# Reordering the first batch of a cross-attention and feed-forward kernel: attention ahead of weights, and idle-time products on the array

## The chip, the cores and the metric

One core of a Trainium2 chip (trn2). The metric is the device time of one execution in microseconds, lower is better. A run of 3 or 5 rounds executes the kernel and the kernel before by turns on the same chip. Runs are compared by their ratios to the kernel before.

## The reference

Eight batches of attention between `x` (8 heads, 512 tokens, 64 wide) and a state of 32 tokens, read in both directions, then a feed-forward block over all 8 x (512 + 32) tokens.

```python
scores = scale * x @ state.T;  a  = softmax(scores);   xread = a @ state      # per batch and head
scores2 = scale * state @ x.T; a2 = softmax(scores2);  sread = a2 @ x
x2 = concat([xread, sread], tokens)            # heads side by side: 512 wide
h  = x2 @ w_in                                 # 512 -> 2048
sp = softplus(h)
out = (h * erf(sp)) @ w_out                    # 2048 -> 512
```

`w_in` and `w_out` come to the kernel as 64-bit numbers, so the kernel must turn them into 32-bit ones itself.

## The kernel before

The weights are loaded in pieces of 1 MB. Each piece costs two ScalarE and three VectorE passes, and these stand among everything else that the first batch asks of the two engines.

```python
def weight(dst, src, shape, tag, bufs):
    raw = act.tile([P, 2 * shape[0] * i], U32, name=tag, bufs=bufs)
    nc.sync.dma_start(out=raw..., in_=src.bitcast(U32))
    lo, hi = words[:, :, 0], words[:, :, 1]
    nc.scalar.activation(out=dst, in_=hi.bitcast(F32), func=ACTF.Copy, scale=2.0 ** -112)
    nc.scalar.activation(out=lo, in_=lo, func=ACTF.Copy, scale=2.0 ** -29)
    nc.vector.tensor_scalar(d, d, 3, None, op0=ALU.logical_shift_left)
    nc.vector.tensor_tensor(d, d, lo, op=ALU.add)
    nc.vector.scalar_tensor_tensor(out=d, in0=hi, scalar=0x80000000, in1=d, ...)

def weights_in(g):                 # two pieces: 256 rows of w_in by 512 columns
    ... weight(..., "raw", 2)
def weights_out(g):                # two pieces; their raw tiles share tag "hs" with hidden()
    ... weight(..., "hs", 2)
```

The attention's output itself is not formed: `mixed` multiplies the states into `w_in` (tile `m`), and `hidden` multiplies the attention weights `aT` by it. A group is four rows of 128 hidden columns.

```python
def hidden(b, fts, t0, n):
    hs = act.tile([P, 4, S], F32, name="hs")
    s = act.tile([P, 4, S], F32, name="s")
    for i in range(4):                                   # four "hidden rows"
        hp = ps_h.tile([P, S], F32, name="h")            # PSUM, two buffers
        ... two matmuls of 128x512 ...
        nc.scalar.activation(out=s[:, i, :], in_=hp, func=ACTF.Softplus)
        nc.vector.tensor_copy(hs[:, i, :], hp)           # frees hp
    nc.scalar.activation(out=s, in_=s, func=ACTF.Erf)
    nc.vector.tensor_tensor(s, s, hs, op=ALU.mult)       # "the product"

load_st(nc.scalar, slice(0, 1))      # eight small loads
load_x(0)                            # eight loads, all on sync's queue
states(0)
rest = attention(0)                  # rest: the read of the states, side work
for b in range(B + 1):
    for g, (first, second) in enumerate(groups):
        if b == 0:
            weights_in(g); mixed(0, g); weights_out(g)
        ...
        gT = first()                 # hidden
        if b == 0 and g == 0:
            rest()
        if pending is not None:
            pending()                # projection of the group before
```

A scheduler settles the order of each engine's instructions; what is written in the program only bounds it.

Of the kernel before, what the change touches and what calls it, by code (L numbers as in the profile page):

```python
# [8 lines left out]
F32 = mybir.dt.float32  # L9
U32 = mybir.dt.uint32  # L10
ALU = mybir.AluOpType
ACTF = mybir.ActivationFunctionType
# [4 lines left out]
def kernel(  # L17
# [17 lines left out]
    nc = tc.nc  # L35
    B, H, S, D = x.shape
    Ns = state.shape[2]
    d_model, d_ff = moe_w_in.shape
    P = 128
    NI = H // 2  # L40
    NC = S // P
    NK = d_model // P
    NF = d_ff // P
    GF = 4
    NG = NF // GF
    TB = S + Ns
    scale = 1.0 / (D ** 0.5)
# [3 lines left out]
    const = ctx.enter_context(tc.tile_pool(name="const", bufs=1))  # L51
# [14 lines left out]
    x_t = {}  # L66


    def load_x(b):
        t = xin.tile([P, NC, H, D], F32, name="x")  # L70
        for h in range(H):
            nc.sync.dma_start(out=t[:, :, h, :], in_=x[b, h].rearrange("(p c) d -> p c d", c=NC))
        x_t[b] = t


    st = const.tile([P, B, P], F32, name="st")

    def load_st(queue, bs):
        for h in range(H):
            i, e = h // 2, h % 2  # L80
            queue.dma_start(out=st[Ns * i:Ns * i + Ns, bs, D * e:D * e + D],
                            in_=state[bs, h].rearrange("b n d -> n b d"))

    load_st(nc.scalar, slice(0, 1))
    load_x(0)

    w_in = const.tile([P, NG, NK, GF * P], F32, name="w_in")
    w_out = const.tile([P, NF, d_model], F32, name="w_out")

    def weight(dst, src, shape, tag, bufs):  # L90
# [20 lines left out]

    gw = GF * P

    def weights_in(g):
        fs = slice(gw * g, gw * g + gw)
        for k in range(0, NK, 2):
            weight(w_in[:, g, k:k + 2, :],
                   moe_w_in[P * k:P * k + 2 * P, fs].rearrange("(k p) f -> p k f", p=P),
                   (2, gw), "raw", 2)

    def weights_out(g):
        for t in range(GF * g, GF * g + GF, 2):
            weight(w_out[:, t:t + 2, :],
                   moe_w_out[P * t:P * t + 2 * P].rearrange("(t p) e -> p t e", p=P),
                   (2, d_model), "hs", 2)


    sT = const.tile([P, NK, B, Ns], F32, name="sT")
# [3 lines left out]
    def states(b):  # L132

        ps = ps_at.tile([P, P], F32, name="at")
        nc.tensor.transpose(out=ps, in_=st[:, b, :], identity=ident)
        stT[b] = keep.tile([P, P], F32, name="stT")
        nc.scalar.copy(stT[b], ps)

    def attention(b):

        xt = x_t.pop(b)
        xT = att.tile([P, NI, S], F32, name="xT")
# [14 lines left out]
                                 start=True, stop=True)  # L157
        sc = att.tile([P, 2, S], F32, name="sc")
        for e in range(2):
            nc.scalar.copy(sc[:, e], s2[e])  # L160

        both = att.tile([P, NI, S], F32, name="xT")
        a = both[:, 0:2].rearrange("p e (k n) -> p e k n", n=Ns)
        aT[b] = keep.tile([P, 2, S], F32, name="aT")
        for e in range(2):
            s1 = ps_at.tile([P, NC * NI, Ns], F32, name="at")
            for c in range(NC):
                nc.tensor.transpose(out=s1[:, NI * c:NI * c + NI, :],  # L168
                                    in_=sc[:, e, P * c:P * c + P], identity=ident)
            m1 = small.tile([P, NC * NI], F32, name="m1")  # L170
            nc.vector.reduce_max(out=m1, in_=s1, axis=AX.X)
            nc.vector.tensor_tensor(a[:, e], s1, m1.unsqueeze(2).to_broadcast([P, NC * NI, Ns]),
                                    op=ALU.subtract)
            nc.scalar.activation(out=a[:, e], in_=a[:, e], func=ACTF.Exp, scale=scale)
            z1 = small.tile([P, NC * NI], F32, name="z1")
            nc.vector.reduce_sum(out=z1, in_=a[:, e], axis=AX.X)
            nc.vector.tensor_scalar(z1, z1, 1e-9, None, op0=ALU.add)
            nc.vector.reciprocal(z1, z1)
            nc.vector.tensor_tensor(a[:, e], a[:, e],
                                    z1.unsqueeze(2).to_broadcast([P, NC * NI, Ns]), op=ALU.mult)  # L180

        for e in range(2):
            ps = ps_at.tile([P, S], F32, name="at")
# [37 lines left out]
            nc.tensor.transpose(out=ps, in_=sn, identity=ident)  # L221
            nc.scalar.copy(sT[:, :, b, :], ps)

        return rest

    m_t = {}

    def mixed(b, g):

        mg = mix.tile([P, 2, gw], F32, name="m")  # L230
        ps = [ps_at.tile([P, gw], F32, name="at") for _ in range(2)]
        for i in range(NI):
            for e in range(2):
                r, q = slice(D * e, D * e + D), slice(Ns * i, Ns * i + Ns)
                nc.tensor.matmul(out=ps[e][q, :], lhsT=stT[b][r, q],  # L235
                                 rhs=w_in[r, g, i, :], start=True, stop=True)
        nc.scalar.copy(mg[:, 0], ps[0])  # L237
        nc.vector.tensor_copy(mg[:, 1], ps[1])  # L238
        m_t[b, g] = mg

    def hidden(b, fts, t0, n):



        hs = act.tile([P, 4, S], F32, name="hs")
        s = act.tile([P, 4, S], F32, name="s")
        m = S // n
        for i in range(4):
            hp = ps_h.tile([P, S], F32, name="h")
            for j in range(m):  # L250
                ops = pairs(b, fts[m * i + j], slice(t0, t0 + n))
                for k, (lhsT, rhs) in enumerate(ops):
                    nc.tensor.matmul(out=hp[:, n * j:n * j + n], lhsT=lhsT, rhs=rhs,  # L253
                                     start=(k == 0), stop=(k == len(ops) - 1))
            nc.scalar.activation(out=s[:, i, :], in_=hp, func=ACTF.Softplus)  # L255
            nc.vector.tensor_copy(hs[:, i, :], hp)  # L256
        nc.scalar.activation(out=s, in_=s, func=ACTF.Erf)  # L257
        nc.vector.tensor_tensor(s, s, hs, op=ALU.mult)  # L258
        return s, hs

    def project(gT, g, acc):
        for r in range(NC):
# [87 lines left out]
    def pairs(b, f, toks):  # L350
        g, fs = f // GF, slice(P * (f % GF), P * (f % GF) + P)
        if b < B:
            return [(m_t[b, g][:, e, fs], aT[b][:, e, toks]) for e in range(2)]
        return [(w_in[:, g, k, fs], sT[:, k].rearrange("p b n -> p (b n)")[:, toks])
                for k in range(NK)]

    def tiles(n):
# [2 lines left out]
    def plain(b):  # L360

        box = []

        def project_(g, gT):
            if g == 0:
                box.extend(tiles(NC))
            project(gT, g, box)
            if g == NG - 1:
                store(box, lambda r, ot: put_x(b, r // 2)(r % 2, ot))
        for g in range(NG):  # L370
            yield lambda g=g: hidden(b, range(GF * g, GF * g + GF), 0, S)[0], \
                lambda gT, g=g: project_(g, gT)

    def fast(b, parts, put):

        for h in range(parts):
            box = []

            def project_(gT, k, g, h, box):
                if k == 0:  # L380
                    box.extend(tiles(4))
                project7(*gT, g, k == 0, k == 1, box)
                if k == 1:
                    store7(box, put(h))
            for k in range(2):
                g = k ^ (h & 1)
                yield lambda g=g, h=h: hidden(b, range(2 * GF * g, 2 * GF * g + 2 * GF),
                                              2 * P * h, 2 * P), \
                    lambda gT, k=k, g=g, h=h, box=box: project_(gT, k, g, h, box)

    states(0)
    rest = attention(0)
    pending = last = None
    for b in range(B + 1):
        if b == 0:
            groups = plain(b)
        elif b < B:
            groups = fast(b, 2, lambda h, b=b: put_x(b, h))
        else:
            groups = fast(b, 1, lambda h: put_s)  # L400
        for g, (first, second) in enumerate(groups):
            if b == 0:
                weights_in(g)
                mixed(0, g)
                weights_out(g)
                if g == 1:
                    load_st(nc.sync, slice(1, B))
            if b + 1 < B and g == (1 if b == 0 else 0):
                load_x(b + 1)
                states(b + 1)  # L410
            gT = first()
            if b == 0 and g == 0:
                rest()
            if pending is not None:
                pending()
            if last is not None:
                last()
                last = None
            if b == 0 and g == NG - 1:
                last = combine_w()  # L420

            def pending(gT=gT, second=second):
                second(gT)
            if b + 1 < B and (b or g):
                for i in [g] if b or g > 1 else [0, 1]:
                    mixed(b + 1, i)
                if g == (NG - 1 if b == 0 else 1):
                    attention(b + 1)()
    pending()


# [28 lines left out]
```

## Time and profile before

| | before |
|---|---|
| median of 3 (lowest to highest) | 817.22 us (816.39 to 817.23) |
| span of the profiled execution | 816.1 us |
| mean granted clock | 0.981 |
| TensorE busy | 784.9 us |
| first projection starts | 55.74 us |

PE is TensorE, DVE is VectorE, ACT is ScalarE. A line of the profile in order of time has the start in us, the busy us, the engine, the source line, the operation, output and input tiles and their sizes, the number of records, and in brackets the idle time before it with what ended that. A matmul of 32-bit numbers leaves two records. The prediction below shows the slices, windows, waits and the start; these lines of the same view (TensorE alone) go beside those of the changed kernel:

```profile
33.46 5.44 PE L253 MATMUL h<-aT,m 128*128 128x512 f32 x8 [0.72 <-ACT m L237]
...
39.45 3.70 PE L253 MATMUL h<-aT,m 128*128 128x512 f32 x8
...
50.56 5.34 PE L253 MATMUL h<-aT,m 128*128 128x512 f32 x8
```

Each line is two hidden rows. They take 3.70 us at full clock; at 33.46 and at 50.56 the clock is at half for most or part of them, 5.44 and 5.34.

### The profile page before, as it was taken

How to read it: one execution, taken by the hardware profiler on the slowest of the kernel's cores; microseconds unless marked ns; L12 is line 12 of the kernel's file. 1: busy time of each engine (PE TensorE's matmuls, PEld its weight loads, DVE VectorE, ACT ScalarE, POOL GpSimd, SP SyncE). 2: the span in 40 equal slices, each digit the busy share in tenths (PEclk: the TensorE clock that was granted, in tenths of full speed). 3: DMA queues.
4: the chain of work that ended last, by engine and by line, in shares of the span. 5: the costliest groups of instructions: out<-in, count | busy, mean ns of one | idle time of the engine just before them, and what ended most of it. 6: DMA issues, size and time to landing. Idle time of an engine off the chain costs nothing.

```text
span 816.1 us, 10344 instructions
## 1 busy us (share of the span) xinstructions
PE 784.9 (96%) x4384; PEld 598.3 (73%) x4384; DVE 429.0 (53%) x625; ACT 370.4 (45%) x465; POOL 0.7 (0%) x6
## 2 busy tenths in 40 slices
PE   4589999999999999999999999999999999999997
PEld 2233434778888788878887888878887788888886
DVE  1979765438444554556453844555454745443431
ACT  4778444545333833345333633373334533333220
POOL 0000000000000000000000000000000000000000
PEclk8589999999999999999999999999999999999999
DMA  7578200202000020002000110000000000000000
GB/s 262 158 231 251 77 27 33 72 1 46 33 1 27 1 78 1 27 1 78 1 27 0 25 55 1 26 1 27 1 26 1 27 1 27 1 27 0 26 1 26
DMA packets 45485, 35.26 MB, mean 43 GB/s; under 512 B 36992, under 2 KB 36992, under 8 KB 45440
## 3 DMA queue, kind: packets, MB, share of 16 engines
q1 hardware_dynamic: 45056, 34.55, 13.6%
q8 instruction: 34, 0.56, 0.3%
q10 hardware_dynamic: 384, 0.07, 0.0%
q14 instruction: 11, 0.09, 0.0%
HBM read 25.69 MB, written 8.91 MB: 42 GB/s over the span
## 4 chain that ended last, share of the span: by engine, by line
PE 88%; ACT 5%; DVE 3%; DMA 3%; issue 1%; SPq 0%
PE o L317 44%; PE h L253 30%; PE at L235 4%; PE o L264 4%; DMA hs<-in_moe_w_out_dram 1%; PE at L168 1%; PE at L146 1%; PE at L185 1%; ACT L255 1%; PE at L202 1%; PE at L214 1%; DMA raw<-in_moe_w_in_dram 1%; ACT s L255 1%; DVE s L258 1%; ACT s L257 0%
## 5 line engine op out<-in xcount | busy, mean ns | idle before, releaser
L253 PE MATMUL h<-aT,m 128*128 128x256 f32 (+1 forms) x960 | 243.4, 401 | 1.9 <-ACT m L237 1.8
L253 PEld LDWEIGHTS h<-aT,m 128*128 128x128 f32 x960 | 178.8, 191 | 67.2 <-issue 33.7
L256 DVE COPY hs<-h 128x512 f32<-128x512 f32 x136 | 93.4, 690 | 198.2 <-ACT s L255 198.2
L255 ACT ACTIVATE s<-h 128x512 f32<-128x512 f32 x136 | 80.3, 597 | 170.9 <-PE h L253 170.5
L258 DVE TENSOR_TENSOR s<-s,hs 128x2048 f32<-128x2048 f32 x34 | 77.9, 2292 | 77.1 <-ACT s L257 77.1
L317 PE MATMUL o<-raw,hs 128*128 128x256 f32 x480 | 115.7, 380 | 0.0
L317 PE MATMUL o<-w_out,s 128*128 128x256 f32 x480 | 115.0, 379 | 0.0
L317 PE MATMUL o<-w_out,hs 128*128 128x256 f32 x480 | 113.4, 379 | 0.0
L317 PEld LDWEIGHTS o<-w_out,hs 128*128 128x128 f32 x480 | 91.2, 190 | 12.4
L317 PEld LDWEIGHTS o<-w_out,s 128*128 128x128 f32 x480 | 90.2, 190 | 12.6 <-DVE s L258 0.8
L317 PEld LDWEIGHTS o<-raw,hs 128*128 128x128 f32 x480 | 90.2, 190 | 12.3
L237 ACT COPY m<-at 128x512 f32<-128x512 f32 x32 | 18.7, 584 | 155.4 <-PE at L235 155.4
L257 ACT ACTIVATE s<-s 128x2048 f32<-128x2048 f32 x34 | 65.0, 1911 | 0.4
L264 PE MATMUL o<-w_out,s 128*128 128x512 f32 x128 | 58.8, 598 | 0.0
L317 PE MATMUL o<-T,s 128*128 128x256 f32 x240 | 56.7, 379 | 0.0
L255 ACT ACT_TABLE_LOAD x41 | 52.6, 1283 | 0.7
L317 PEld LDWEIGHTS o<-T,s 128*128 128x128 f32 x240 | 45.1, 190 | 5.9
L238 DVE COPY m<-at 128x512 f32<-128x512 f32 x32 | 22.1, 690 | 45.6 <-PE at L235 45.5
L264 PEld LDWEIGHTS o<-w_out,s 128*128 128x128 f32 x128 | 23.4, 190 | 30.4 <-issue 30.3
L257 ACT ACT_TABLE_LOAD x34 | 43.6, 1283 | 0.6
L235 PE MATMUL at<-w_in,stT 64*32 64x512 f32 x512 | 41.6, 630 | 0.9 <-ACT m L237 0.5
L328 ACT COPY m<-o 128x256 f32<-128x256 f32 x15 | 5.6, 372 | 57.7 <-PE o L317 57.7
(71 smaller groups left out, 556.4 us busy)
## 6 DMA issues: line engine op xcount, KB each, us to landing
x<-in_x_dram SPq DMA_DIRECT2D x64, 128.0 KB, 3.1
raw<-in_moe_w_in_dram SPq DMA_DIRECT2D x8, 1024.0 KB, 6.1
hs<-in_moe_w_out_dram SPq DMA_DIRECT2D x8, 1024.0 KB, 5.0
out_dram<-ot SPq DMA_DIRECT2D x32, 256.0 KB, 2.4
out_dram<-ot SPq DMA_DIRECT2D x8, 64.0 KB, 1.7
st<-in_state_dram SPq DMA_DIRECT2D x8, 56.0 KB, 4.9
st<-in_state_dram ACTq DMA_DIRECT2D x8, 8.0 KB, 2.1
```

What stands on the lines that cost most here:

```text
L146: nc.tensor.transpose(out=xp[:, P * c:P * c + P], in_=xt[:, c, 2 * i:2 * i + 2, :], identity=ident)
L168: nc.tensor.transpose(out=s1[:, NI * c:NI * c + NI, :], in_=sc[:, e, P * c:P * c + P], identity=ident)
L235: nc.tensor.matmul(out=ps[e][q, :], lhsT=stT[b][r, q], rhs=w_in[r, g, i, :], start=True, stop=True)
L237: nc.scalar.copy(mg[:, 0], ps[0])
L238: nc.vector.tensor_copy(mg[:, 1], ps[1])
L253: nc.tensor.matmul(out=hp[:, n * j:n * j + n], lhsT=lhsT, rhs=rhs, start=(k == 0), stop=(k == len(ops) - 1))
L255: nc.scalar.activation(out=s[:, i, :], in_=hp, func=ACTF.Softplus)
L256: nc.vector.tensor_copy(hs[:, i, :], hp)
L257: nc.scalar.activation(out=s, in_=s, func=ACTF.Erf)
L258: nc.vector.tensor_tensor(s, s, hs, op=ALU.mult)
L264: nc.tensor.matmul(out=acc[r], lhsT=gT[:, i, P * r:P * r + P], rhs=w_out[:, GF * g + i, :], start=(g == 0 and i == 0), stop=(g == NG - 1 a ...
L317: nc.tensor.matmul(out=acc[bank][:, E2 * c:E2 * c + E2], lhsT=lhs[:, i, :], rhs=rhs[:, g, i, :], start=(first and i == 0 and c == 0), stop ...
```

## The change

The intent is to shorten the start: x comes on two queues; attention goes ahead of the weights' conversions by fixed orders; `w_in` comes in pieces that hold all rows of 256 columns, so that half a mixed product needs one piece; thirty products that nobody reads keep the array busy; the side work `rest()` goes from the first group to the third.

```diff
-    def load_x(b):
+    def load_x(b, queues=(nc.sync,)):
...
+    for e in range(2):
+        nc.sync.dma_start(out=st[:, 0, D * e:D * e + D], in_=state[0].rearrange(...)[e])
+    load_x(0, (nc.scalar, nc.sync))
-    load_st(nc.scalar, slice(0, 1))
-    load_x(0)
...
-    def weights_in(g):           # two pieces per group, each 256 rows x 512 columns
+    def weights_in(j):           # one piece: 512 rows x 256 columns
...
+    def warm(n):
+        for _ in range(n):
+            nc.tensor.matmul(out=spare[:, 0:P], lhsT=ident, rhs=ident, start=True, stop=True)
...
+    def begin(on_pe, on_act, on_dve):        # called in attention, behind the subtractions
+        with tc.issue_after(on_pe.ins):
+            warm(20)
+        with tc.issue_after(on_act.ins), tc.issue_after(on_dve.ins):
+            weights_in(0)
+
+    warm(10)
     states(0)
-    rest = attention(0)
+    rest, on_act, on_dve = attention(0, begin)
+    with tc.issue_after(on_act.ins), tc.issue_after(on_dve.ins):
+        weights_in(1)
+    on_act, on_dve = mixed(0, 0, 2)
+    with tc.issue_after(on_act.ins), tc.issue_after(on_dve.ins):
+        weights_out(0)
...
-            gT = first()
-            if b == 0 and g == 0:
-                rest()
+            before, gT = gT, first()
+            if b == 0 and g == 2:
+                with tc.issue_after(before[2].ins):
+                    rest()
```

Cut: the loop's bookkeeping, `mixed` in parts, and the later loads of x and states. `issue_after` sets an order on an engine, not a wait for the result.

## The prediction

> **What bounds the kernel now.** I read the page's forty slices first, then busy time in 20 us windows, then what TensorE waited for, then the start in order of time. Slices (one is 20.4 us):
>
> ```profile
> PE   4589999999999999999999999999999999999997
> DVE  1979765438444554556453844555454745443431
> ACT  4778444545333833345333633373334533333220
> PEclk8589999999999999999999999999999999999999
> ```
>
> TensorE is full from the fourth slice on; only the first three have room, and there its clock is low and VectorE is at 9, 7, 9. Windows (columns: stretch and length, busy us of PE, PEld, DVE, ACT, POOL, clock, DMA share, GB/s):
>
> ```profile
> 0.00:20.00 20.00, 8.52 (x41) 4.84 (x41) 3.30 (x4) 8.45 (x12) 0.70 (x6) 0.83 0.80 266
> 20.00:40.00 20.00, 11.44 (x39) 4.73 (x39) 19.31 (x31) 14.31 (x18) 0.00 (x0) 0.58 0.47 146
> 40.00:60.00 20.00, 17.74 (x112) 7.47 (x111) 15.89 (x20) 15.62 (x20) 0.00 (x0) 0.83 0.80 246
> 60.00:80.00 20.00, 19.15 (x75) 6.75 (x73) 18.35 (x20) 16.84 (x17) 0.00 (x0) 1.00 0.78 247
> ```
>
> TensorE is idle 11.48 + 8.56 + 2.26 = 22.3 us before 60 us. From 20 to 40 VectorE works 19.31 of 20. TensorE's waits up to 130 us:
>
> ```profile
> PE at L185 <- DVE xT L179: 7.7, 2, 7.0
> PE at L135 <- DMA st<-in_state_dram: 6.6, 1, 6.6
> PE at L156 <- ACT xT L148: 3.8, 1, 3.8
> PE h L253 <- ACT m L237: 1.8, 2, 1.1
> ```
>
> And the start:
>
> ```profile
> 13.85 1.12 ACT L105 ACTIVATE w_in<-raw 128x1024 f32<-128x1024 f32 x1 [3.51 <-DMA raw<-in_moe_w_in_dram]
> 14.86 0.58 ACT L148 COPY xT<-at 128x512 f32<-128x512 f32 x1
> 17.49 1.07 ACT L160 COPY sc<-at 128x512 f32<-128x512 f32 x2 [1.00 <-PE at L156]
> 20.75 1.28 DVE L172 TENSOR_TENSOR xT<-at,m 128x512 f32<-128x512 f32 x2
> 38.08 0.60 ACT L255 ACTIVATE s<-h 128x512 f32<-128x512 f32 x1 [0.28 <-PE h L253]
> 48.26 2.29 DVE L258 TENSOR_TENSOR s<-s,hs 128x2048 f32<-128x2048 f32 x1 [1.32 <-ACT s L257]
> 55.74 2.74 PE L264 MATMUL o<-w_out,s 128*128 128x512 f32 x6
> ```
>
> The reader sees ScalarE held 3.51 us by a weight transfer while the last xT copy stands behind it; the first Softplus at 38.08; the first projection at 55.74. After that TensorE lacks only 0.39 + 0.46 + 1.11 + 0.48 us up to 140.
>
> **The Trainium skill.** "TensorE: Matmul & The Clock Gate", Part 1, says the array runs at half clock after a little-used window of about 3.4 us, full after a busy one, the windows running freely. The trace agrees: full to 13.1, half to 37.0, full to 47.2, half to 54.0, distances of 7, 3 and 2 times 3.41. The same page (Architectural detail) says ScalarE and VectorE queues are strictly first in, first out; the 3.51 us above is that. "DMA: Bandwidth & Descriptors" (Issuing engines are not separate DMA queues) says a second issuer saves only issue time; here eight x issues take 6.51 us on one queue, so issue is what limits x. "ScalarE: Activation LUTs" (What ACT_TABLE_LOAD costs) gives 1283 ns; the page's rows show 1283.
>
> **The change, part by part.** I compared the order of instructions on each engine and which instruction each wait is for. From the second batch on the orders are the same, so only the first batch can move. As units I take distances from one start to the next in the trace: ScalarE conversion 1.02 (two per 1 MB piece), VectorE's three per piece 0.60 + 1.13 + 1.13 = 2.86, copies and reductions 0.60, a hidden matmul instruction 0.86 at full clock and 1.72 at half, a 1 MB load 5.07 from issue to landing.
>
> x on two queues, state in two loads instead of eight. Four x issues go on ScalarE (0.65 each, done by 3.3), four on sync behind two state loads; two of these wait for an earlier transfer's semaphore, so the last x lands near 8.1 (3.1 after issue) against 10 now. The first w_in piece follows it by 3.9 as now: 12.0.
>
> Attention ahead. Last xT copy 8.75 instead of 14.86, scores copied at 10.4 to 11.4, both subtractions done at 14.05 instead of 22.03: eight us won. But the fixed order only says "not before"; the built order puts the first piece's two ScalarE conversions (12.0 to 14.1) before the exponentials, and its three VectorE passes between the sums. Chain: exponentials 14.1 to 15.2, pass 14.0, sum, pass 15.3, sum, pass 17.1, scalings to 20.1. Two transposes and aT copies end near 22.3 (now 30.7).
>
> Finer w_in. The first mixed half needs one piece, but its two sides use one PSUM buffer in turn: m halves ready near 22.4 and 23.7, hidden matmuls from about 23.1 (now 33.46). ScalarE must convert the third piece first: its raw buffer comes free at 18.4, so landed 23.5, converted 25.5, table 26.8. The three hidden matmuls ahead of the second mixed half end at about 28.1 at half clock. First Softplus there, ten us earlier than 38.08.
>
> Here the gain is given back. w_out's two pieces, converted before the first hidden matmul now, come after the mixed copies, and the hidden copy needs a buffer which they hold. From T = 28.1: Softplus and m copy to 29.1, four ScalarE conversions to 33.2, VectorE behind them (third and second-last passes), first hs copy ended at 35.9. The third hidden row can't start before; TensorE idles about 6 us, falls to half clock, and ends row four near 42.0. Softplus, one w_out conversion, table, Erf: 42.7, 43.7, 45.0, 46.9; the product ends at 49.2 (now 50.55). The next m copy stands behind Erf, so group two's hidden matmuls start at 47.5 (now 50.56), four at half clock rising midway: first projection near 53.5, or 51.2 if the clock stays up.
>
> Side work later. rest() goes from group one to group three: the same 2.0 us on TensorE (eight transposes 0.87, sixty-four small products 1.03, one transpose 0.11), but out of the starved stretch.
>
> Idle-time products. Thirty 128-column products are two passes of 0.108 each: 6.5 us, ten before 3.5, twenty from 12.1 to 16.4. Both lie in idle time, and nothing waits for them. They keep the clock to 17 or 20, where little runs; not to 36 or 47, where it would pay.
>
> Sum. TensorE's useful work at full clock before the first projection is 19.1 now (0.1 state, 4.5 attention, 1.0 + 1.0 mixed, 6.9 + 3.45 hidden, 2.0 rest, 0.1 next state), so 55.74 - 19.1 = 36.6 lost. Changed: 17.0 done by 53.5, 36.5 lost; 34.2 at best. Win 0 to 2.4. Later waits: 2.4 now; changed about 0.7 (a hidden row behind a combine subtraction of 2.3) and 2.7 in the last group (m copies behind the last w_out piece, whose load starts only after the product, 5.07 + 2.04 later, then behind another subtraction), 0.5 at the next attention: 3.9. So +1.5 worse to 0.9 better; I take 1 us off this as some waits may overlap: 816.
>
> **Rivals.** (1) The whole early win stays: the first Softplus ten us earlier becomes ten us less, some 807. For it: nothing after 60 us is starved, so what is won at the first projection is kept. Against: VectorE's sum. Before the first hs copy it has about five pieces less one pass, 13.2, plus attention and copies 8.5; from 11.5 that ends at 33.2 with no gap at all, and TensorE has work for only two rows till then. (2) The clock is the cause: the products hold it up to the hidden matmuls, 51.2 instead of 53.5, so 814. For it: at half clock a hidden row costs double, and the kernel now runs 23.9 + 6.8 us so. Against: a near-idle array from 16.4 to 19.3, and little until 23. (3) Weights arrive late: if the first piece lands at 13.8 as now, exponentials stand behind it and all moves 1.8: 818. For it: x and weights share the same transfer engines, at 409 GB/s from 10 to 15. (4) A wait in the last group of batch one grows, w_out loads behind x loads in the sync queue: 820.
>
> **Range and chances.** 2% is 16.3 us, nearly half of the 36.6 lost; VectorE's sum lets the third hidden row start at 33.2 at the earliest against 39.45 now, so even a stretch without gaps wins about 6 there. 816 with 809 to 820: the low end keeps most of rival 1, the high end is rival 4. Faster by 2%: 0.03; within: 0.95; slower: 0.02.
>
> **What would show it.** Right: last xT copy near 9, exponentials 14 to 15, first Softplus near 28 and then a gap of 5 to 7 us on TensorE put to the hs copy; w_out conversions between first and second Softplus; first projection 51 to 54; clock at half again before 24; same idle time after 160. Wrong: Softplus two begins right after one, first projection before 49, or full clock from 20 to 50. Then the order of conversions cost less than I count, and the time is nearer 808.

## The result, and the profile after

A ratio below is the mean time of one kernel's fast runs over that of the other's of the same rounds, so it is not quite the ratio of the medians that are quoted.

| | before | changed |
|---|---|---|
| median of 4 | 817.23 us | 817.49 us (817.17 to 819.43) |
| ratio to before, 95% interval | | 1.0011 (0.9993 to 1.0028) |
| span, mean clock | 816.1, 0.981 | 815.4, 0.988 |
| first projection | 55.74 | 53.48 |

The same time, within 0.3%. The slices of the changed kernel's page (one slice 20.4 us):

```profile
PE   7679999999999999999999999999999999999997
DVE  3899545438454644556453844555454745443431
PEclk9699999999999999999999999999999999999999
```

And its 20 us windows, with the columns that the prediction names:

```profile
0.00:20.00 20.00, 14.82 (x101) 12.02 (x101) 7.07 (x13) 10.26 (x14) 0.70 (x6) 1.00 0.92 280
20.00:40.00 20.00, 12.46 (x52) 4.84 (x53) 17.56 (x24) 13.52 (x15) 0.00 (x0) 0.69 0.78 209
40.00:60.00 20.00, 15.66 (x46) 6.43 (x45) 18.29 (x21) 16.33 (x17) 0.00 (x0) 0.88 0.73 253
60.00:80.00 20.00, 20.00 (x129) 9.07 (x127) 19.93 (x24) 17.17 (x21) 0.00 (x0) 1.00 0.41 137
```

The first slice is fuller by the products and the earlier attention, but the third has gone from 8 to 7. TensorE is idle 5.2 + 7.5 + 4.3 = 17.1 us before 60, against 22.3. The products themselves take 4.34 (the ten, at half clock) + 4.63 us, and together with the idle time that is 26.0: more than before. What fell is the time at half clock by the record, 17.0 us now (20.9 to 27.7, 34.5 to 41.3, 48.1 to 51.5) against 30.7. (The record counts the time up to its first change as full clock; see the end.) VectorE works 17.56 + 18.29 + 19.93 = 55.8 of the 60 us from 20 to 80, before 53.6.

What TensorE waited for up to 130 us (total, times, longest):

```profile
PE h L269 <- DVE hs L272: 7.0, 2, 6.4
PE h L269 <- ACT m L255: 3.1, 1, 3.1
PE at L195 <- DVE xT L190: 2.7, 1, 2.7
```

The seven us for attention's scalings (`xT`) are down to 2.7. A new wait of 6.4 for a copy of `hs` stands at the top. In order of time:

```profile
9.79 0.59 ACT L156 COPY xT<-at 128x512 f32<-128x512 f32 x1 [0.26 <-PE at L154]
14.85 1.23 ACT L185 ACTIVATE xT<-xT 128x512 f32<-128x512 f32 x2
...
29.42 0.60 ACT L271 ACTIVATE s<-h 128x512 f32<-128x512 f32 x1
...
30.16 1.22 ACT L108 ACTIVATE w_out<-hs 128x1024 f32<-128x1024 f32 x1
...
34.29 0.61 ACT L271 ACTIVATE s<-h 128x512 f32<-128x512 f32 x1
...
36.44 0.68 DVE L272 COPY hs<-h 128x512 f32<-128x512 f32 x1
...
37.27 5.68 PE L269 MATMUL h<-aT,m 128*128 128x512 f32 x8 [6.45 <-DVE hs L272]
...
48.38 5.26 PE L269 MATMUL h<-aT,m 128*128 128x512 f32 x8 [3.08 <-ACT m L255]
53.48 2.74 PE L279 MATMUL o<-w_out,s 128*128 128x512 f32 x6
```

The last xT copy is five us earlier than before, the exponentials are at 14.85, the first Softplus is nine us earlier. Then ScalarE converts `w_out` from 30.16, and its second Softplus starts at 34.29. VectorE reaches the first `hs` copy at 36.44, behind its own passes over `w_out`. Row three starts at 37.27, before at 39.45: of nine us two are left. The fall of the clock that the wait brings makes rows three and four 5.68 instead of 3.70, and group two's rows start 2.2 us earlier than before.

The first projection is 2.26 us earlier, and yet the time is the same. The 2.0 us of side work that stood before it now come after it, and the waits after it are 0.4 us less (below). That leaves 2.26 - 2.0 + 0.4 = 0.7 us, the difference of the two spans, 816.1 and 815.4. So nearly all that the start shows as gain is work that was moved.

### The profile page after: what moved, and what is told of

The parts are those of the page before. It is cut to its first block, busy times and chain, and to the rows that moved or that the text cites. A ratio compares the mean times of both kernels' runs of the same rounds, so it can differ in the third digit from the quotient of the medians.

```text
span 815.4 us, 10488 instructions
## 1 busy us (share of the span) xinstructions
PE 790.0 (97%) x4460; PEld 605.4 (74%) x4460; DVE 428.6 (53%) x626; ACT 369.4 (45%) x465; POOL 0.7 (0%) x6
## 3 DMA queue, kind: packets, MB, share of 16 engines
q1 hardware_dynamic: 45256, 34.09, 13.6%
## 4 chain that ended last, share of the span: by engine, by line
PE 83%; ACT 3%; DVE 3%; DMA 1%; issue 1%
PE o L332 45%; PE h L269 27%; PE at L253 3%; PE o L279 3%; PE at L154 1%; PE at L177 1%; ACT L271 1%; PE at L212 1%; PE at L224 1%; PE at L195 1%; ACT s L271 1%; DVE s L274 1%; DMA hs<-in_moe_w_out_dram 1%; DVE raw L301 1%; ACT s L273 0%
## 5 line engine op out<-in xcount | busy, mean ns | idle before, releaser
L255 ACT COPY m<-at 128x512 f32<-128x512 f32 (+1 forms) x33 | 18.9, 571 | 158.2 <-PE at L253 158.2
L271 ACT ACT_TABLE_LOAD x40 | 51.3, 1283 | 0.7
L255 DVE COPY m<-at 128x512 f32<-128x512 f32 (+1 forms) x33 | 22.2, 673 | 47.3 <-PE at L253 47.3
L273 ACT ACT_TABLE_LOAD x34 | 43.6, 1283 | 0.6
L253 PE MATMUL at<-w_in,stT 64*32 64x512 f32 (+1 forms) x528 | 39.6, 595 | 2.1 <-DVE w_in L112 1.3
```

Source lines behind the costliest of these rows:

```text
L253: nc.tensor.matmul(out=ps[e][q, :], lhsT=stT[b][r, q], rhs=w_in[r, fs, i, :], start=True, stop=True)
L255: return nc.scalar.copy(mg[:, 0], ps[0]), nc.vector.tensor_copy(mg[:, 1], ps[1])
```

## The experiments

All twelve ran with five rounds; the kernel before had medians of 817.5, 817.35, 817.5 and 816.6. Where an experiment takes something from the changed kernel without moving the rest, every engine's order was held as it was built there (dependencies between neighbours that add no wait), so that the scheduler could not answer with another order. The first run checks that this costs nothing. The theory: the early gain is given back because `w_out`'s conversions stand between Softplus and `hs` copies, and the clock and the products matter little. The main rival: the array's clock sets the first 55 us.

| run | median us | ratio to before | 95% | first projection |
|---|---|---|---|---|
| e1_same | 818.52 | 1.0023 | 1.0008 to 1.0039 | 54.70 |
| e2_no_products | 820.20 | 1.0035 | 1.0022 to 1.0047 | 56.41 |
| e3_hold_clock | 816.86 | 0.9996 | 0.9984 to 1.0009 | 50.90 |
| e4_wout_after | 814.98 | 0.9973 | 0.9959 to 0.9987 | 48.39 |
| e5_high_words | 814.64 | 0.9972 | 0.9956 to 0.9988 | 53.88 |
| e6_x_alone | 816.31 | 0.9985 | 0.9960 to 1.0011 | 51.39 |
| e7_side_work_early | 817.80 | 1.0012 | 0.9997 to 1.0026 | 53.43 |
| e8_wout_spread | 814.81 | 0.9972 | 0.9959 to 0.9985 | 45.49 |
| e9_x_again | 816.00 | 0.9983 | 0.9967 to 1.0000 | 52.40 |
| e10_x_hold_second | 814.97 | 0.9970 | 0.9958 to 0.9982 | 53.06 |
| e11_x_hold_both | 812.69 | 0.9942 | 0.9930 to 0.9954 | 50.16 |
| e12_hold_alone | 814.50 | 0.9975 | 0.9961 to 0.9989 | 52.66 |

The first projection is that of the one profiled execution. It shifts by about a microsecond between executions of one order (the changed kernel 53.48, its control 54.70) as the first transfers land earlier or later. In e6, e7 and e9 to e11 it comes after one hidden row of the second group, in the others after two; a row takes some 1.7 us at full clock, so these two sets are not to be compared with each other. e4_wout_after, e6_x_alone and e7_side_work_early were not held: the scheduler could order them anew.

### e1_same: the control

```diff
+    ORDER = {"PE": [...], "DVE": [...], "Activation": [...], "SP": [...]}   # as built
+    for engine, runs in ORDER.items():
+        for a, b in zip(line, line[1:]):
+            tc.add_manual_dep(b, a.name, no_sync, reason="frozen order")
```

> The changed kernel once more, with every engine's order written down and enforced, as the control for the runs with edits. All theories: the same program order, so 817.5 within 0.5 us, first Softplus near 29.4, first projection near 53.5.

818.52 us, half a microsecond above the expected range; every instruction in its old place. The waits are the same, all some 1.2 us later from the first x on, which landed later in the profiled execution:

```profile
26.25 4.15 PE L275 MATMUL h<-aT,m 128*128 128x512 f32 x6
...
38.42 5.73 PE L275 MATMUL h<-aT,m 128*128 128x512 f32 x8 [6.37 <-DVE hs L278]
```

By ratio it is 0.12% above the changed kernel, and the two intervals overlap: so much two runs of one order differ.

### e2_no_products: the thirty products away

```diff
-    warm(10)
-            warm(20)
```

> The changed kernel without the thirty idle-time products, every other order kept. Theory A (the conversions on VectorE and ScalarE ahead of the first hs copy set the pace; the products lie in idle time): within 1 us of the control, first projection 53 to 54. Theory B (TensorE's clock sets the pace of the first 55 us): the array is at half clock for its scores and its transposes too, so 2 us or more slower, first projection 55 or later.

820.2 us, by ratio 0.12% and by medians 1.7 us over the control; the two intervals overlap, and 0.12% is also what lies between the control and the changed kernel. This falls between the two expectations. Rows one and two took 5.43 us instead of 4.15 for the records shown together, rows three and four 6.35 instead of 5.73; the wait before row three stayed, 6.43. By the record the clock is at half from 17.3 to 31.0 without the products, from 22.1 to 28.9 with them. The later rise need not come from the products: e7_side_work_early has all thirty, and its clock rose at 30.0 and its rows took 5.40. So what thirty products are worth, nothing or a microsecond, is not shown.

```profile
25.75 5.43 PE L274 MATMUL h<-aT,m 128*128 128x512 f32 x6
```

### e3_hold_clock: products in all the waits

```diff
-    warm(10) ... warm(20)
+    fill = {0: warm(10), 33: warm(31), 41: warm(1), 45: warm(2), 61: warm(36), 65: warm(13), 73: warm(12)}
```

The numbers ahead of the colons are places in TensorE's order.

> The changed kernel with 105 instead of 30 idle-time products, placed in the gaps that its trace shows before 48 us so that the clock stays full, every other order kept. Theory A: hidden rows one and two end some 2 us earlier and it does no good (the third row still begins near 37.3), rows three and four save nothing either since the next w_out load lands near 43.4, only group two's rows at full clock are worth 1.7 us: first projection 51.5 to 52.5, time 815.5 to 817. Theory B: each of the three half-clock stretches gives back its half, 3.4 + 3.4 + 1.7 us: first projection before 48, time 812 or less.

816.86 us; the record shows full clock throughout. TensorE in order of time:

```profile
28.27 8.20 PE L133 MATMUL o<-ident 128*128 128x128 f32 x72
36.54 3.67 PE L275 MATMUL h<-aT,m 128*128 128x512 f32 x8
```

The wait is now filled with products, and rows one and two take 2.84 us instead of 4.15 for the records shown together, but row three starts at 36.54, 1.9 earlier than the control's 38.42 and within a microsecond of the changed kernel's own 37.27. So what it waits for isn't the array. The rival asked for 812 or less, and at that size it falls. The first projection, at 50.90, is 3.8 us before the control's, between the two expectations, and 1.7 us of that reach the end (0.27% by ratio). But the control has thirty of these products already. From no products at all (e2_no_products) to a full clock it is 3.3 us, 0.39%, about what e4_wout_after gains. So the theory's second half, that the clock and the products matter little, does not hold for the two together.

### e4_wout_after: the first w_out conversions behind group two's mixed copies

The raw tiles of `w_out`'s first group go to buffers that lie free (the second x tile, and the place of a tile used later), so that they need no `hs` buffer, and the conversions come later in the order.

```diff
-        raw = act.tile([...], U32, name=tag, bufs=bufs)
+        pool = {"x": xin, "T4": const}.get(tag)
+        raw = pool.tile([...], U32, name=tag) if pool is not None else act.tile(...)
...
-                   (2, d_model), "hs", 2)
+                   (2, d_model), "hs" if g else ("T4" if t % GF else "x"), 2)
...
-    with tc.issue_after(on_act.ins), tc.issue_after(on_dve.ins):
-        weights_out(0)
...
-                mixed(0, g)
+                on_act, on_dve = mixed(0, g)
+                if g == 1:
+                    with tc.issue_after(on_act.ins), tc.issue_after(on_dve.ins):
+                        weights_out(0)
```

> The changed kernel with the first two w_out pieces in buffers of their own (the second x buffer and the one that is used later for the combined weights), converted only after group two's mixed copies, so that the first hs copy waits for nothing but its Softplus. Theory A: third hidden row from near 31 instead of 37.3, product of group one ends near 42 instead of 50.2, first projection 46 to 48, time 4 to 7 us under the control (810.5 to 813.5), if the won time is not lost again to the loads of the last group. Theory B: the array is still cold in the gaps, so the third row starts earlier but the projection comes less than 3 us earlier.

814.98 us, 3.5 under the control and 2.5 under the kernel before. TensorE:

```profile
32.09 3.67 PE L271 MATMUL h<-aT,m 128*128 128x512 f32 x8 [1.38 <-DVE hs L274]
...
48.39 6.28 PE L281 MATMUL o<-w_out,s 128*128 128x512 f32 x14 [1.82 <-DVE w_out L114]
```

Row three starts five us earlier, after 1.38 us instead of 6.45, and at full clock. The first projection then waits 1.82 us for the conversions that were put off, and is still 5 to 6 us earlier. That shows the step of the prediction in which the gain is given back. Of 6.3 us at the first projection (control 54.70), 3.5 reach the end (4.4 between the two profiled executions). The edit moves several things at once: the buffers, the place of the conversions and, as the second x tile is taken, the next batch's loads of x, issued from 48.4 on instead of 27 to 39. Which of buffer and place the first `hs` copy needed was not tested apart.

### e5_high_words: conversions without their low words

```diff
-        nc.scalar.activation(out=lo, in_=lo, func=ACTF.Copy, scale=2.0 ** -29)
-        nc.vector.tensor_tensor(d, d, lo, op=ALU.add)
```

> The changed kernel in its own order, but each weight is made from the high word of its double alone: in every conversion the second ScalarE pass (1.14 us) and the second VectorE pass (1.22 us) are left out, 16 and 16 instructions. The weights lose their lowest mantissa bits, on purpose. Theory A (the conversions on ScalarE and VectorE set the first 55 us, because rows three and four wait behind them): the wait before the third hidden row falls from 6.4 us to below 4.5, the first projection starts 4 to 6 us earlier than the control's 54.7, the time is 812.5 to 815. Theory B (the transfers of the weights or the clock of the array set it): the first projection is within 1.5 us of 54.7 and the time is 816.5 to 819.

814.64 us, some 4 us under the control by ratio, but the first projection of the profiled execution (816.43, the longest of its six) is only 0.8 earlier. Row three starts at 35.61 instead of 38.42. Then:

```profile
47.82 6.23 PE L273 MATMUL h<-aT,m 128*128 128x512 f32 x8 [4.97 <-ACT m L259]
```

Group two's rows wait five us for the copy of `m`, which stands behind Erf. Erf stands behind a `w_out` conversion for whose transfer ScalarE waited 1.33 us, until 42.95. Neither expectation holds whole: the time agrees with the first, the start with the second. A lighter engine in the same order runs into the next thing that it stands behind, here a transfer. Most of the time's gain came after the start, and which wait it came from was not looked into further.

### e6_x_alone: the kernel before, with the new loads of x and of the states

```diff
-    load_st(nc.scalar, slice(0, 1))
-    load_x(0)
+    for e in range(2):
+        nc.sync.dma_start(out=st[:, 0, D * e:D * e + D], in_=state[0].rearrange(...)[e])
+    load_x(0, (nc.scalar, nc.sync))
```

> The kernel before with one thing of the change: x of batch 0 on two queues and the first states in two loads. Theory A (an earlier x carries through to the end): the last xT copy moves from 14.9 to about 10 us, the first projection from 55.7 to 53.5 to 54.5, the time is 815.5 to 816.5. Theory B (what attention gains is given back at the weights, which VectorE and ScalarE still convert in their old order): attention ends 3 to 5 us earlier, the first projection moves by less than 1 us, the time is 817 to 818.5.

816.31 us, but the six times are 812.0, 813.6 and 814.6, and 818.0, 818.2 and 818.9. The profiled one (813.6) has its first projection at 51.39, although its xT copies still stand behind a weight conversion (last one at 14.27, not near 10 as expected, and at 14.98 in e9_x_again; 14.86 in the kernel before). The first hidden rows start no earlier, at 33.64 here and 34.53 in e9_x_again, against 33.46. So it is not the earlier x that carries through. What differs is the order that the scheduler built for it: the side work stands otherwise between the hidden rows, and the projection starts after one row of the second group instead of two. "x on two queues" below means the loads with that order; they were not tested apart. In the profiled execution the clock is at full from 38 us on; the second fall of the kernel before (47.2 to 54.0) isn't there.

### e7_side_work_early: the changed kernel with rest() back in the first group

```diff
-            if b == 0 and g == 2:
-                with tc.issue_after(before[2].ins):
-                    rest()
+            if b == 0 and g == 0:
+                rest()
```

> The changed kernel with the read of the states (2 us of TensorE and its copies on ScalarE and VectorE) back at the first group, where the kernel before has it, instead of the third. Theory A (moving it later takes VectorE and ScalarE work out of the stretch that they bound): first projection 2 to 3 us later than the control's, time 820 to 822. Theory B (it lies in waits of TensorE there and costs nothing, so that moving it later gains nothing): first projection within 1 us of the control's, time 817.5 to 819.5, with the 2 us of TensorE paid in one place or the other.

817.8 us, first projection 53.43, after one row of the second group. Five of the nine transposes lie at the wait before row three, which is there anyway; the rest of the side work stands from 44.46 to 47.4, and group two's rows start at 50.16 instead of 48.38. So some 1.8 of its 2.0 us are paid in the start and saved later: they are paid in one place or the other, as the second expectation has it. Moving the side work gained nothing that these runs can tell.

### e8_wout_spread: w_out's conversions in idle stretches, and the clock held

From e4_wout_after, by editing the held orders: ScalarE's four passes over the first `w_out` group go before the first copy of `m`, where ScalarE was idle 5.4 us; VectorE's six passes go into its gaps and behind the first product; 78 products (the text on record says 75) stand in the waits up to the second group's rows.

> The version with w_out of the first group staged apart, and three orders more: its ScalarE passes stand in ScalarE's idle 5.4 us before the first copy of m, its VectorE passes in VectorE's idle stretches and behind the first product, and 75 idle-time products keep the array clocked between 9 and 38 us. Theory A (conversion order and clock are what is left): third row at 29 to 31 us (32.1 in the staged version), first projection at 44.5 to 46.5 (48.4), time 811.5 to 813.5. Theory B (the 1 MB transfers, 2.9 us apart, bind by now): first projection at 47.5 or later, time 814 to 815.5.

Row three at 30.50 and the first projection at 45.49, as the first theory has it, but 814.81 us, the same as e4_wout_after. The three us won are lost again after 50: 1.76 us before group two's third row, and then (ScalarE and TensorE in order of time)

```profile
94.86 1.12 ACT L110 ACTIVATE w_out<-hs 128x1024 f32<-128x1024 f32 x1 [7.50 <-DMA hs<-in_moe_w_out_dram]
...
96.51 1.09 PE L261 MATMUL at<-w_in,stT 64*32 64x512 f32 x14 [2.32 <-ACT m L263]
```

ScalarE stands 7.5 us at a conversion whose transfer has not landed, with the copy of `m` behind it that TensorE needs. VectorE has 54.8 us of work between 20 and 80 here, and 52 to 56 of these 60 us in every version that converts whole words: a faster array reaches the same conversions earlier and waits for them.

### e9_x_again and e10_x_hold_second: does a second fall of the clock make the long runs?

```diff
+    fill = {97: warm(5), 102: warm(3)}       # e10; e9: none
```

> The kernel of the run with x alone once more, every engine's order held as it was there: a control, because that run's times lay in two groups, 812 to 815 and 818 to 819, and its profile caught a fast one (span 811.8) in which the clock fell only once in the first 100 us. Theory A (the two groups differ by a second fall of the clock near 47 us, which the kernel before shows from 47.2 to 54.0): the times spread over 812 to 819 again; if the profile catches a run over 817, its windows between 44 and 58 us show granted shares of 0.5 and a span of 815 or more; if it catches one under 815, they show 1.00. Theory B (the two groups come from something else, such as when transfers land): the clock in these windows is the same in a long run as in a short one, and waits of TensorE differ.

> The same with eight products on the array in its two idle stretches between 45 and 48.5 us (5 of 0.227 us before the transpose of the read states, where it waited 1.2 us, and 3 between the two banks of the mixed copies, where it waited 0.9 us). Theory A (a second fall of the clock makes the long runs): all times 812 to 815, median 812.5 to 814, granted share 1.00 between 44 and 58 us. Theory B: still two groups, median 815 to 817.5.

e9: 814.5, 814.7 and 814.9, and 817.1, 817.3 and 817.7; the profile caught a short one again (814.94), again with full clock from 44 to 58. With the eight products, five runs of 814.3 to 816.2, median 814.97. So the upper group is gone and the lower one no shorter. That fits the second fall as the cause of the long runs, but no long run was ever profiled: it stays likely, not shown. The mean clocks on record separate the groups of e6 and e9 too, but not as a second fall on top of the first would: 0.992 to 0.995 in the six long runs, 0.985 to 0.989 or 1.00 in the short ones. As the next lines show, the record can count a long stretch at half clock as full, so this decides nothing. The expected 812.5 to 814 was too low by a microsecond.

This profile also shows how far the clock's record goes. The slices of e10, and TensorE's first two hidden rows:

```profile
PEclk9999999999999999999999999999999999999999
```

```profile
34.19 6.50 PE L268 MATMUL h<-aT,m 128*128 128x512 f32 x8 [1.48 <-ACT m L252]
```

A clock of 0.9 or more throughout, while two rows take 6.50 us that take 3.70 at full clock. The durations say that the array was at half clock from its first instructions: four transposes of x took 1.09 us at 6.68, eight of the scores 1.97 at 17.64, where e11_x_hold_both has 1.14 for those eight. No change came before the first rise, and until then the record reads full.

### e11_x_hold_both: products in every wait up to 48 us

```diff
+    fill = {0: warm(10), 13: warm(13), 25: warm(3), 33: warm(31), 37: warm(3), 49: warm(7), 97: warm(5), 102: warm(3)}
```

> The same with products in the earlier waits too (10 at the start, 13 before the last x transposes, 3, 31, 3 and 7 in the waits between 17 and 33.5 us, and the eight of the run above), so that the clock need not fall at all before 60 us. Theory A (before the first projection VectorE and ScalarE set the pace, so a faster array only waits longer): the first four hidden rows take 3.7 to 4 us less of TensorE, but the first projection starts less than 1.5 us earlier than in the run with eight products, and the time is within 1.5 us of it. Theory B (TensorE at half clock sets the first 55 us): first projection at 47 to 49, time 809 to 811.

812.69 us (812.60 to 813.78), 0.58% under the kernel before, the best of all and the steadiest. The page's slices and TensorE in order of time:

```profile
PE   7899999999999999999999999999999999999997
```

```profile
18.86 7.09 PE L119 MATMUL o<-ident 128*128 128x128 f32 x62
...
34.09 3.70 PE L268 MATMUL h<-aT,m 128*128 128x512 f32 x8 [0.94 <-ACT m L252]
...
50.16 1.02 PE L279 MATMUL o<-w_out,s 128*128 128x512 f32 x2
```

The 7 us wait for attention is full of products, the first rows start as late as ever (34.09), but run at 3.70, and the first projection is 2.9 us earlier than in e10, the time 2.3 shorter. That is outside what the first theory allows (1.5) and short of what the second asks (809 to 811). In this order, where `w_out` is converted before the first row and row three waits for nothing, the clock does set part of the start.

### e12_hold_alone: the products alone, in the kernel before

```diff
+    fill = {0: warm(12), 20: warm(14), 25: warm(3), 33: warm(30), 37: warm(3), 49: warm(3), 81: warm(3), 97: warm(6)}
```

> The kernel before in its own order, with 74 products in TensorE's waits before 47 us (12 at the start, 14, 3, 30, 3, 3, 3 and 6), and nothing else: x stays on one queue. Theory A (what holding the clock is worth does not depend on the earlier x: with x on two queues it took 3.3 us off): first four hidden rows 3.6 to 3.7 us each two instead of 5.4, both falls of the clock gone, first projection at 51 to 53 instead of 55.7, time 813 to 814.8. Theory B (the clock matters only where attention has been brought forward): first projection later than 54, time 816 to 817.5.

814.5 us, 0.25% under the kernel before. Rows one and two took 3.70 us from 30.55 on; row three then waited 2.0 us for an `hs` copy, and rows three and four took 5.17 between them. So a faster array meets the conversions here too, and part of its gain becomes a wait. First theory for the time, near its upper end, but rows three and four missed their 3.7.

## Why the prediction was right

It put 816, with 809 to 820, and the change within 2% at 0.95; the changed kernel has 817.49. (The middle of its "+1.5 worse to 0.9 better", less 1 us, is 816.5.) By its steps:

- **Attention earlier: right, one to two microseconds too early throughout.** Last xT copy 9.79 (8.75 predicted), second subtraction done at 15.4 (14.05), exponentials from 14.85 (14.1), first hidden matmul 25.05 (23.1), first Softplus 29.42 (28.1). The first x landed at 6.69 and the last xT copy ran a microsecond late, and everything behind it kept that or lost a little more.
- **The gain given back: right, and shown.** Softplus and conversions in the order that it named, 6.45 us idle for "about 6", row three at 37.27 for 35.9, the product ended at 50.18 for 49.2, first projection 53.48 for 53.5. That the last is exact is luck: group two's rows started 0.9 us late (48.38 for 47.5) and took 5.1 us for 6.0. Its own units, two matmuls at 1.72 and two at 0.86, give 5.2 for a rise midway, so from 47.5 its sum is 52.7 and not 53.5. e4_wout_after moves those conversions and gets row three at 32.09 and 3.5 us at the end.
- **Side work later: right in effect.** Its 2.0 us are out of the starved stretch and are paid after it. e7_side_work_early, with the side work back in the start, takes the same time.
- **Idle-time products: right on the clock (20.9 for "17 or 20"); their worth is open.** It set them at nothing; without them it is 1.7 us by the medians and 0.12% by ratio, with intervals that overlap.
- **The clock's record: misread at its start.** It took the clock as full to 13.1. The first twelve transposes of x took 2.85 us from 6.86 on, and four took 0.63 at 10.10: the array was at half clock for the first ones. Little hangs on it.
- **Later waits: mis-sized.** 3.9 us were expected after the first projection, some 2.0 are there (0.53 + 0.38 + 0.30 + 0.59 + 0.20), less than the 2.44 before. The last group's copies of `m` waited little; in e8_wout_spread, which comes to them earlier, that wait is there with 2.3 us.
- **Rival 1**, the whole gain staying, falls with e4_wout_after: even with row three freed, 2.5 us under the kernel before, not 10. **Rival 2**, the clock, is worth 2 us in the changed order over the thirty products that are in it (e3_hold_clock), as it was put there. Counted from no products it is 3.3 us in the changed order (e2 to e3), 3.3 with x on two queues (e9 to e11) and 2.1 in the kernel before (e12_hold_alone). **Rivals 3 and 4** did not come.

The parts can be added up, by ratios. x on two queues, with its order, is -0.16% (mean of e6 and e9; their intervals reach 0), the products as placed -0.12% (not clear of noise), the side work nothing. The changed kernel is at +0.11 to +0.23%. So the new order with its finer pieces would cost some 0.4 to 0.5%, or 3 to 4 us, and e4_wout_after, which repairs one place of it, gains 0.50%. Each term is uncertain by 0.15% or more, and that the terms add up is assumed: that the order costs is worked out from the sum, not measured alone. Of the finer pieces alone no run was made, so how much they gain or cost stays open.

## What to carry to other kernels

When work is put forward on an engine that is nearly full (VectorE here, 52 to 56 of the 60 us from 20 to 80), look for what moves behind it, and for the buffer that the displaced work and the next stage share: that is where the gain goes. Ask of each early microsecond which instruction on the way to the end waits for it. When a gain shows at one point of the trace, ask which work was moved behind that point: here 2.0 of 2.3 us. Products that hold the array's clock took 2 to 3 us off in three orders, also in the one where a conversion is waited for; compare such gains from the same start, with no products in either. Try the small parts of a change one by one, as the best version here is the two small ones (x on two queues and a held clock) without the large one.

## What the Trainium skill lacked or had wrong

- **"TensorE: Matmul & The Clock Gate", Part 1 and Part 4.** Part 1 warns that clock events in a trace are unreliable. These runs show one shape of it: until the first event the record reads 1.00 at half clock. The first products took 0.434 us each under a record of 1.00, the later ones 0.227, and in e10_x_hold_second it reads full for the whole of the first 39 us (6.50 us for rows that take 3.70). Part 4 says that the full clock doesn't engage for transposes, which it does not count as busy in the same way; here four of them took 0.63 us where the clock was held and 1.09 where it was not (the transposes of `xT` in e11 and e9), so they run at the granted clock. They also seem to raise it: in the kernel before, only transposes had run on the array (the first twelve of x in 2.85 us) when the next four took 0.63 at 10.10.
- **"ScalarE: Activation LUTs", What ACT_TABLE_LOAD costs.** The page gives 1283 ns and a drain of 1380 ns for each switch, 2.66 us in all. The load took 1.28 us here, and the next activation began 0.02 us after it ended (28.12 + 1.28, then 29.42), and the one before it had ended at 28.11; no drain is to be seen in its neighbourhood.
- **No page has it:** what products that nobody reads are worth when they hold the clock through the waits of a start: 3.3 us of some 817 in two orders (e2 to e3, e9 to e11) and 2.1 in a third (e12_hold_alone).
